# Decoding the third weight group over three steps instead of one, in a fused attention and two-MLP kernel

## The chip, the cores and the metric

The kernel runs on one core of one Trainium2 chip. The metric is the device time of one execution in microseconds; the median of several runs counts. The engines are PE (TensorE, matmuls), DVE (VectorE), ACT (ScalarE), POOL (GpSimd) and SP (SyncE, which issues nearly all DMA transfers). Each works through its own queue in order; between engines they wait on semaphores.

## What is computed

The reference is attention with 4 batches, 8 heads, 576 positions and a head size of 64; heads 0 to 3 see the last 32 positions, heads 4 to 7 every 32nd position. Its output, 2304 tokens by 512, goes through two MLPs:

```
x = attention(q, k, v)                      # 2304 x 512
gate = 1 / (1 + exp(-(x @ w_gate)))         # 512 -> 1536
x = (gate * (x @ w_val)) @ w_out            # 1536 -> 512
h = x @ w_in                                # 512 -> 2048
out = softplus(h) @ w_out2                  # 2048 -> 512
```

All in float32. The kernel splits each float32 operand of the MLPs into a high and a low part and takes three matmuls (high x high, high x low, low x high) for each product.

## The kernel before

**Tiles and loops.** The 2304 tokens are five blocks t = 0 to 4, of 512 tokens and the last of 256. The hidden units of both MLPs are cut into 14 groups g of 256: groups 0 to 5 are the first MLP, with three weight matrices each (m = 0 gate, 1 value, 2 out), groups 6 to 13 the second, with two. A step is a pair (g, t). In `step` (L261) a step of the first MLP sends PE the gate product of this block (`gates`, L161), then the down product of the step before (`down`, L258, and `out1`, L188), then the value product (`values1`, L175); every generator yields after three matmuls, and such a step has 24 yields: 8 gates, 8 down, 8 values. Behind the gates ACT computes a sigmoid for each of two columns (L171). Behind the values DVE multiplies by it (L184, sg), ACT rounds to the high part (L151, gh), DVE takes the low part (L152, gl); the next step's down product reads gh and gl. The down products are taken out of PSUM by ACT in group 0 (L202), by DVE in the others (L204, addition to the accumulator). In PSUM the gate and value products share four buffers, the down products another four.

**Weights.** They come from memory as 64-bit words. A piece (g, m, c) is one half of a matrix, 512 KB; `load_next` (L92) issues its DMA on SP into one of three buffers `raw` and puts the piece into `queue`; `todo` holds the pieces still to be loaded. `decode_steps` (L101) turns the next piece of the queue into its high and low part: two DVE instructions make f (L108, L112), two make e (L117, L122), ACT copies f into the high tile (L121), POOL subtracts (L125) and adds (L126) to make the low tile. Then it calls `load_next`. f and e have two buffers each. There are two sets of weight tiles, taken in turn: group g lies in set g % 2, so tile w00h is the high part of set 0, matrix 0. A piece of group 2 can only be written once its tile has been read for the last time by group 0.

**Order around the change.** The order on every engine is the order in which the code emits instructions. Groups 0 and 1 are taken together: during attention the steps (0,0), (1,0), (0,1), ... (1,2), which fill PE between pieces of attention; then the list `rest` (L271): (0,3), (0,4), (1,4), (1,3), and from there group by group, (2,0) to (13,4). The loop at L543 walks through `rest`, and at a yield j with j % 3 == 2 it may emit one decode. Before the change, `free` allows decodes in (1,3) (all pieces of group 2, six) and, for later groups, from block 1 on (an even share for each step). The pieces of `todo` for groups from 2 on are ordered half by half: all matrices of half 0, then of half 1 (L329). Fifteen pieces are loaded in the attention part, so the first three of group 2 are there early; each later load is issued by a decode.

Of the kernel before, what the change touches and what calls it, by code (L numbers as in the profile page):

```python
# [24 lines left out]
NCC = DM // P  # L25
# [9 lines left out]
GC = 2  # L35
# [7 lines left out]
def tile_sparse_attention_moe_moe2(  # L43
# [17 lines left out]
    NB = len(blocks)  # L61
    NBA = B - 1
    NG = NG1 + NG2
# [23 lines left out]
    queue, todo = [], []  # L87

    def group_mats(g):
        return (0, 1, 2) if g < NG1 else (0, 2)  # L90
# [39 lines left out]
    def decode_next(pools):  # L130
        for _ in decode_steps(pools):
            pass
# [125 lines left out]
    def down(g, t, pools):  # L258
        return (out1 if g < NG1 else out2)(g, t, pools)

    def step(prev, cur, pools, interleave=False):  # L261
        g, t = cur
        if g < NG1:
            yield from gates(g, t, pools, interleave)
            if prev:
                yield from down(*prev, pools)
            yield from values1(g, t, pools)
        else:
            yield from step2(prev, cur, pools)
# [4 lines left out]
    def attention():  # L274
        with ExitStack() as actx:
# [42 lines left out]
            def load_v(i):  # L318
# [7 lines left out]
            todo.extend([(0, 0, 0), (0, 0, 1), (0, 1, 0), (0, 1, 1), (1, 0, 0), (1, 0, 1)])  # L326
            todo.extend([(0, 2, 0), (0, 2, 1), (1, 1, 0), (1, 1, 1), (1, 2, 0), (1, 2, 1)])
            todo.extend(
                (g, m, c) for g in range(2, NG) for c in range(GC) for m in group_mats(g)  # L329
            )  # L330
            load(1)
            load(2)
# [27 lines left out]
            for h in range(2):  # L360
                t = m_loc[h * LQ:(h + 1) * LQ]
# [3 lines left out]
            t = m_str[:SQ].rearrange("p (a b) -> p a b", a=RG)  # L365
# [141 lines left out]
            for u in range(NU + SKEW):  # L507
                t, pos = divmod(u - START, PB)
# [8 lines left out]
                n = 0  # L517
# [12 lines left out]
    with tc.manual_schedule():  # L530
        attention()

        late = ctx.enter_context(tc.tile_pool(name="late", bufs=1))
        pool = lambda name, bufs, **kw: ctx.enter_context(tc.tile_pool(name=name, bufs=bufs, **kw))
        pools = {
            "g": pool("gp2", 2), "t": pool("tp2", 3), "d": pool("decp2", 2), "e": nc.gpsimd,
            "h": pool("ps_h2", 4, space=PSUM), "y": pool("ps_y2", 4, space=PSUM),
        }
        for t in range(NBA, NB):
            acc[t] = late.tile([P, NCC * blocks[t][1]], F32, name=f"acc{t}")  # L540

        prev = (1, NBA - 1)
        for i, cur in enumerate(rest):  # L543
            g, t = cur
            free = (g == 1 and t == 3) or (g > 1 and t > 0)
            n = 0
            if free:
                left = sum(pc[0] == g + 1 for pc in queue + todo)
                n = left if g == 1 else -(-left // max(NB - 1 - t, 1))
            for j, _ in enumerate(step(prev, cur, pools)):  # L550
                if n and j % 3 == 2:
                    n -= 1
                    decode_next(pools)
            while n:
                n -= 1
                decode_next(pools)
            prev = cur
        for _ in down(*prev, pools):
            pass
# [81 lines left out]
```

## Time and profile before

| | |
|---|---|
| runs, us | 983.05, 982.62, 980.76; median 982.62 |
| profiled execution: its time on the core, from first to last instruction (span) | 978.8 us |
| PE busy | 952.3 us (97%) |
| DVE busy | 609.3 us (62%) |
| ACT busy | 404.2 us (41%) |
| POOL busy | 284.1 us (29%) |
| DMA, bytes moved | 62.27 MB, mean 64 GB/s |

For the profiled execution only the span is listed, not the device time of the run around it; the median of the runs lies 3.8 us above this span. Shares of busy time are averages over the whole span; the steps differ, and a stretch is read best from a table of busy times by step and from the engines' timelines.

### The profile page before, as it was taken

To read this page: it belongs to the slowest core of one execution; us is meant where nothing else is said; L and a number is where in the kernel's file an instruction comes from. 1 tells how busy PE (TensorE), PEld (TensorE's weight loads), DVE (VectorE), ACT (ScalarE), POOL (GpSimd) and SP (SyncE) were. 2 spreads that over 40 slices of the span, in tenths; PEclk is the share of its full clock that TensorE was granted. 3 is DMA by queue.
4 is the path that set the end of the run, shared out by engine and by line. 5 is a ranking of instruction groups with operands and counts; after the bars stand their busy time and mean duration, and the time that the engine had idled before them with its cause. 6 is when DMAs were issued, how large, how long until landed. Compare 5 with 4: busy or idle time off the path is not lost.

```text
span 978.8 us, 13104 instructions
## 1 busy us (share of the span) xinstructions
PE 952.3 (97%) x5148; PEld 787.3 (80%) x5148; DVE 609.3 (62%) x969; ACT 404.2 (41%) x729; POOL 284.1 (29%) x256
## 2 busy tenths in 40 slices
PE   8879999999989999999999999999999999999998
PEld 6757778788768888888888887888888888888886
DVE  5888854412767637637636448484859584858554
ACT  3446656642212212212113355454545454455443
POOL 6555533310424204203305534040403031313100
PEclk9979999999979999999999999999999999999999
DMA  8665633100312102102202002020202010200023
GB/s 250 189 194 150 183 98 90 32 7 1 85 45 71 59 1 68 63 1 65 65 1 65 22 1 85 2 76 11 67 20 65 22 64 22 65 22 22 1 78 116
DMA packets 24795, 62.27 MB, mean 64 GB/s; under 512 B 2975, under 2 KB 7071, under 8 KB 24735
## 3 DMA queue, kind: packets, MB, share of 16 engines
q1 hardware_dynamic: 24672, 61.44, 20.7%
q8 instruction: 40, 0.66, 0.3%
q14 instruction: 20, 0.16, 0.1%
q10 hardware_dynamic: 63, 0.01, 0.0%
HBM read 56.71 MB, written 4.72 MB: 63 GB/s over the span
## 4 chain that ended last, share of the span: by engine, by line
PE 87%; DVE 7%; ACT 2%; DMA 1%; issue 1%; POOL 1%; SPq 0%; POOLq 0%; DVEq 0%
PE ps_y L67 12%; PE ps_y L69 12%; PE ps_y L68 11%; PE ps_h L67 6%; PE ps_h L69 6%; PE ps_h L68 6%; PE ps_v L67 5%; PE ps_v L68 5%; PE ps_v L69 5%; PE ps_g L67 4%; PE ps_g L69 4%; PE ps_g L68 4%; DVE f L112 2%; PE ps_s L382 2%; PE ps_o L444 2%; DVE f L108 1%
## 5 line engine op out<-in xcount | busy, mean ns | idle before, releaser
L151 ACT ACTIVATE gh<-sg 128x512 fp32r<-128x512 f32 (+1 forms) x140 | 82.5, 589 | 254.2 <-DVE sg L184 182.9
L253 DVE TENSOR_TENSOR acc<-ps_y,acc 128x512 f32<-128x512 f32 x126 | 86.7, 688 | 89.1 <-PE ps_y L69 88.1
L152 DVE TENSOR_TENSOR gl<-sg,gh 128x512 fp32r<-128x512 f32 (+1 forms) x140 | 100.3, 716 | 54.6 <-ACT gh L151 51.1
L204 DVE TENSOR_TENSOR acc<-ps_y,acc 128x512 f32<-128x512 f32 (+1 forms) x100 | 61.7, 634 | 67.0 <-PE ps_y L69 67.0
L184 DVE TENSOR_TENSOR sg<-ps_v,sg 128x512 f32<-128x512 f32 (+1 forms) x60 | 38.1, 635 | 84.7 <-PE ps_v L69 84.5
L125 POOL TENSOR_TENSOR f<-f,w00h 128x512 f32<-128x512 f32 x12 | 18.5, 1540 | 212.2 <-ACT w00h L121 212.2
L112 DVE SCALAR_TENSOR_TENSOR f<-raw,f 128x512 uint32<-128x512 uint32 x68 | 74.3, 1093 | 2.3
L225 ACT ACTIVATE sg<-ps_h 128x512 f32<-128x512 f32 (+1 forms) x80 | 43.8, 547 | 64.4 <-PE ps_h L69 64.4
L125 POOL TENSOR_TENSOR f<-f,w10h 128x512 f32<-128x512 f32 x12 | 18.3, 1526 | 154.6 <-ACT w10h L121 154.6
L68 PE MATMUL ps_h<-xl,w00h 128*128 128x512 f32 (+1 forms) x160 | 58.9, 368 | 0.0
L67 PE MATMUL ps_h<-xh,w00h 128*128 128x512 f32 (+1 forms) x160 | 58.9, 368 | 0.0
L69 PE MATMUL ps_h<-xh,w00l 128*128 128x512 f32 (+1 forms) x160 | 58.9, 368 | 0.0
L69 PE MATMUL ps_h<-xh,w10l 128*128 128x512 f32 (+1 forms) x160 | 58.9, 368 | 0.0
L68 PE MATMUL ps_h<-xl,w10h 128*128 128x512 f32 (+1 forms) x160 | 58.8, 368 | 0.0
L67 PE MATMUL ps_h<-xh,w10h 128*128 128x512 f32 (+1 forms) x160 | 58.8, 368 | 0.0
L67 PE MATMUL ps_y<-w02h,gh 128*128 128x512 f32 x144 | 56.6, 393 | 0.7 <-ACT gh L151 0.7
L233 DVE SCALAR_TENSOR_TENSOR sg<-ps_h,sg 128x512 f32<-128x512 f32 (+1 forms) x80 | 50.5, 631 | 11.0 <-ACT sg L227 10.6
L67 PE MATMUL ps_y<-w12h,gh 128*128 128x512 f32 x144 | 56.5, 393 | 0.1
L69 PE MATMUL ps_y<-w02h,gl 128*128 128x512 f32 x144 | 56.5, 392 | 0.0
L69 PE MATMUL ps_y<-w12h,gl 128*128 128x512 f32 x144 | 56.5, 392 | 0.0
L68 PE MATMUL ps_y<-w02l,gh 128*128 128x512 f32 x144 | 56.2, 390 | 0.0
L68 PE MATMUL ps_y<-w12l,gh 128*128 128x512 f32 x144 | 56.2, 390 | 0.0
(115 smaller groups left out, 2538.6 us busy)
## 6 DMA issues: line engine op xcount, KB each, us to landing
raw<-in_w_dram SPq DMA_DIRECT2D x68, 512.0 KB, 3.8
out_dram<-acc SPq DMA_DIRECT2D x18, 256.0 KB, 2.0
qt<-in_q_dram SPq DMA_DIRECT2D x8, 324.0 KB, 4.7
qt<-in_q_dram SPq DMA_DIRECT2D x8, 320.0 KB, 4.5
qt<-in_q_dram SPq DMA_DIRECT2D x8, 270.0 KB, 3.9
qt<-in_q_dram SPq DMA_DIRECT2D x8, 256.0 KB, 3.6
vt<-in_vl_dram SPq DMA_DIRECT2D x8, 240.0 KB, 4.8
vt<-in_vl_dram SPq DMA_DIRECT2D x8, 192.0 KB, 3.5
```

The lines of the kernel that those rows point to most:

```text
L67: nc.tensor.matmul(ps, lhsT=lh, rhs=rh, start=first, stop=False)
L68: nc.tensor.matmul(ps, lhsT=lh, rhs=rl, start=False, stop=False)
L69: nc.tensor.matmul(ps, lhsT=ll, rhs=rh, start=False, stop=last)
L112: nc.vector.scalar_tensor_tensor(out=f, in0=high, scalar=0xC0000000, in1=f, op0=ALU.bitwise_and, op1=ALU.bitwise_or,)
L125: pools["e"].tensor_tensor(out=ff, in0=ff, in1=hi.bitcast(F32), op=ALU.subtract)
L151: nc.scalar.activation(out=gh[:, c, 0:n], in_=src, func=AF.Copy)
L152: nc.vector.tensor_tensor(out=gl[:, c, 0:n], in0=src, in1=gh[:, c, 0:n].bitcast(F32), op=ALU.subtract)
L184: nc.vector.tensor_tensor(out=sg, in0=ps[:, 0:n], in1=sg, op=ALU.mult)
L204: nc.vector.tensor_tensor(out=y, in0=ps[:, 0:n], in1=y, op=ALU.add)
L225: nc.scalar.activation(out=sg, in_=ps, func=AF.Abs)
L233: nc.vector.scalar_tensor_tensor(out=sg, in0=ps, scalar=0.0, in1=sg, op0=ALU.max, op1=ALU.add)
L253: nc.vector.tensor_tensor(out=y, in0=ps, in1=y, op=ALU.add)
```

## The change

The condition `free` is replaced. In (0,4) two decodes are emitted, from yield 8 on (behind the gates of that step, at yields 8 and 11); in (1,4) two, at yields 2 and 5; in (1,3) what is left, two, at yields 2 and 5. For later groups the rule and the places stay the same. In `todo` the pieces from group 2 on go matrix by matrix: both halves of a matrix, then the next matrix.

```diff
--- before.py
+++ after.py
@@ -326,7 +326,7 @@
             todo.extend([(0, 0, 0), (0, 0, 1), (0, 1, 0), (0, 1, 1), (1, 0, 0), (1, 0, 1)])
             todo.extend([(0, 2, 0), (0, 2, 1), (1, 1, 0), (1, 1, 1), (1, 2, 0), (1, 2, 1)])
             todo.extend(
-                (g, m, c) for g in range(2, NG) for c in range(GC) for m in group_mats(g)
+                (g, m, c) for g in range(2, NG) for m in group_mats(g) for c in range(GC)
             )
             load(1)
             load(2)
@@ -542,13 +542,16 @@
         prev = (1, NBA - 1)
         for i, cur in enumerate(rest):
             g, t = cur
-            free = (g == 1 and t == 3) or (g > 1 and t > 0)
-            n = 0
-            if free:
-                left = sum(pc[0] == g + 1 for pc in queue + todo)
-                n = left if g == 1 else -(-left // max(NB - 1 - t, 1))
+            left = sum(pc[0] == g + 1 for pc in queue + todo)
+            n, first = 0, 0
+            if (g, t) == (0, NB - 1):
+                n, first = GC, GC * NCC
+            elif g == 1:
+                n = GC if t == NB - 1 else left
+            elif g > 1 and t > 0:
+                n = -(-left // max(NB - 1 - t, 1))
             for j, _ in enumerate(step(prev, cur, pools)):
-                if n and j % 3 == 2:
+                if n and j >= first and j % 3 == 2:
                     n -= 1
                     decode_next(pools)
             while n:
```

How this moves instructions, at three places. In the names, f, e and raw belong to a decode; 128x256 are instructions of block 4; acc_2454 and acc_2455 are the accumulators of blocks 3 and 4.

DVE between the values of (0,3), whose last gl is of 128x512, and those of (1,4). Before, in this place:

```order
L184 TENSOR_TENSOR sg<-ps_v,sg 128x512
L152 TENSOR_TENSOR gl<-sg,gh 128x512
L184 TENSOR_TENSOR sg<-ps_v,sg 128x256
L152 TENSOR_TENSOR gl<-sg,gh 128x256
L184 TENSOR_TENSOR sg<-ps_v,sg 128x256
L152 TENSOR_TENSOR gl<-sg,gh 128x256
```

Now:

```order
L122 SCALAR_TENSOR_TENSOR e<-raw,e 128x512
L108 TENSOR_SCALAR f<-raw 128x512
L112 SCALAR_TENSOR_TENSOR f<-raw,f 128x512
L117 TENSOR_SCALAR e<-f 128x512
L122 SCALAR_TENSOR_TENSOR e<-raw,e 128x512
L184 TENSOR_TENSOR sg<-ps_v,sg 128x256
L152 TENSOR_TENSOR gl<-sg,gh 128x256
L184 TENSOR_TENSOR sg<-ps_v,sg 128x256
L152 TENSOR_TENSOR gl<-sg,gh 128x256
L108 TENSOR_SCALAR f<-raw 128x512
```

The first row is the end of the first decode of (0,4); the second decode follows whole, then the values of (0,4), then the first decode of (1,4). Before, only values stood in this place.

DVE at the end of (1,3), where its values (L184, L152 of 128x512) end the stretch. Before:

```order
L122 SCALAR_TENSOR_TENSOR e<-raw,e 128x512
L204 TENSOR_TENSOR acc_2455<-ps_y,acc_2455 128x256
L108 TENSOR_SCALAR f<-raw 128x512
L112 SCALAR_TENSOR_TENSOR f<-raw,f 128x512
L117 TENSOR_SCALAR e<-f 128x512
L122 SCALAR_TENSOR_TENSOR e<-raw,e 128x512
L184 TENSOR_TENSOR sg<-ps_v,sg 128x512
L152 TENSOR_TENSOR gl<-sg,gh 128x512
```

Now:

```order
L122 SCALAR_TENSOR_TENSOR e<-raw,e 128x512
L108 TENSOR_SCALAR f<-raw 128x512
L112 SCALAR_TENSOR_TENSOR f<-raw,f 128x512
L117 TENSOR_SCALAR e<-f 128x512
L122 SCALAR_TENSOR_TENSOR e<-raw,e 128x512
L204 TENSOR_TENSOR acc_2455<-ps_y,acc_2455 128x256 x4
L184 TENSOR_TENSOR sg<-ps_v,sg 128x512
L152 TENSOR_TENSOR gl<-sg,gh 128x512
L184 TENSOR_TENSOR sg<-ps_v,sg 128x512
```

The last decode stood between the additions of the down product and the first sg of (1,3); now all four additions and the values follow the last decode together.

ACT from the evictions of (0,4)'s down product on. Before:

```order
L202 ACTIVATE acc_2454<-ps_y 128x512 x4
L151 ACTIVATE gh<-sg 128x256 x2
L171 ACTIVATE sg<-ps_g 128x256 x2
L202 ACTIVATE acc_2455<-ps_y 128x256 x4
L151 ACTIVATE gh<-sg 128x256 x2
L121 ACTIVATE w00h<-f 128x512
L171 ACTIVATE sg<-ps_g 128x512
L121 ACTIVATE w01h<-f 128x512
L171 ACTIVATE sg<-ps_g 128x512
L121 ACTIVATE w02h<-f 128x512
L121 ACTIVATE w00h<-f 128x512
L121 ACTIVATE w01h<-f 128x512
```

Now:

```order
L121 ACTIVATE w00h<-f 128x512
L202 ACTIVATE acc_2454<-ps_y 128x512 x2
L121 ACTIVATE w00h<-f 128x512
L202 ACTIVATE acc_2454<-ps_y 128x512 x2
L151 ACTIVATE gh<-sg 128x256 x2
L121 ACTIVATE w01h<-f 128x512
L171 ACTIVATE sg<-ps_g 128x256
L121 ACTIVATE w01h<-f 128x512
L171 ACTIVATE sg<-ps_g 128x256
L202 ACTIVATE acc_2455<-ps_y 128x256 x4
L151 ACTIVATE gh<-sg 128x256 x2
L121 ACTIVATE w02h<-f 128x512
```

The copies L121 now stand between the evictions L202 of (0,4), and ahead of each of the two sigmoids L171 of (1,4); for (1,3) two are left, both of w02h, of which the last row is the first.

## Rows read from the trace of the kernel before

**Rows 1.** The page: its first line, and the granted clock in 40 slices.

```profile
span 978.8 us, 13104 instructions
...
PEclk9979999999979999999999999999999999999999
```

**Rows 2.** Busy us by step: length, PE, PEld, DVE, ACT, POOL, then clock, DMA.

```profile
229.70:240.74 11.04, 11.04 (x73) 10.08 (x73) 2.07 (x4) 4.21 (x8) 0.00 (x0) 1.00 0.01 1
240.74:249.38 8.64, 8.64 (x75) 8.64 (x74) 1.70 (x5) 3.14 (x8) 0.00 (x0) 1.00 0.00 0
249.38:263.18 13.80, 13.80 (x74) 11.89 (x73) 12.97 (x18) 3.28 (x6) 7.58 (x6) 1.00 0.34 83
263.18:291.10 27.92, 21.58 (x73) 15.79 (x72) 18.97 (x24) 4.76 (x8) 9.87 (x7) 0.82 0.22 73
291.10:307.42 16.32, 16.32 (x73) 13.51 (x72) 11.62 (x16) 3.50 (x6) 5.83 (x4) 1.00 0.20 65
```

**Rows 3.** PE's timeline at the step (2,0): start us, us, engine, line, operands.

```profile
266.13 0.39 PE L68 MATMUL ps_g<-xl,w00h 128*128 128x512 f32 x1
268.72 0.79 PE L69 MATMUL ps_g<-xh,w00l 128*128 128x512 f32 x1 [2.20 <-POOL w00l L126]
...
276.02 0.79 PE L67 MATMUL ps_y<-gh,w12h 128*128 128x512 f32 x1 [3.15 <-ACT gh L151]
277.77 0.80 PE L68 MATMUL ps_y<-gl,w12h 128*128 128x512 f32 x1 [0.96 <-DVE gl L152]
```

**Rows 4.** DVE's timeline, steps (0,3) to (2,0).

```profile
231.11 0.69 DVE L152 TENSOR_TENSOR gl<-sg,gh 128x512 fp32r<-128x512 f32 x1 [0.70 <-ACT gh L151]
239.57 0.42 DVE L184 TENSOR_TENSOR sg<-ps_v,sg 128x256 f32<-128x256 f32 x1 [7.76 <-PE ps_v L69]
240.48 0.43 DVE L152 TENSOR_TENSOR gl<-sg,gh 128x256 fp32r<-128x256 f32 x1 [0.48 <-ACT gh L151]
...
241.85 0.42 DVE L152 TENSOR_TENSOR gl<-sg,gh 128x256 fp32r<-128x256 f32 x1 [0.48 <-ACT gh L151]
...
250.83 0.42 DVE L108 TENSOR_SCALAR f<-raw 128x512 uint32<-128x512 uint32 x1
...
253.08 1.52 DVE L108 TENSOR_SCALAR f<-raw 128x512 uint32<-128x512 uint32 x1
...
257.40 1.52 DVE L108 TENSOR_SCALAR f<-raw 128x512 uint32<-128x512 uint32 x1
...
274.62 0.68 DVE L184 TENSOR_TENSOR sg<-ps_v,sg 128x512 f32<-128x512 f32 x1
276.00 1.72 DVE L152 TENSOR_TENSOR gl<-sg,gh 128x512 fp32r<-128x512 f32 x1 [0.70 <-ACT gh L151]
```

**Rows 5.** POOL's timeline, steps (1,3) and (2,0).

```profile
252.77 1.53 POOL L125 TENSOR_TENSOR f<-f,w00h 128x512 f32<-128x512 f32 x1 [45.16 <-ACT w00h L121]
254.39 1.36 POOL L126 TENSOR_TENSOR w00l<-f,e 128x512 fp32r<-128x512 f32 x1
257.04 1.60 POOL L125 TENSOR_TENSOR f<-f,w01h 128x512 f32<-128x512 f32 x1 [1.29 <-ACT w01h L121]
...
275.90 1.26 POOL L126 TENSOR_TENSOR w02l<-f,e 128x512 fp32r<-128x512 f32 x1
```

**Rows 6.** PE's timeline: the first down product in (1,4), and in (1,3).

```profile
243.62 0.28 PE L67 MATMUL ps_y<-gh,w02h 128*128 128x256 f32 x1
...
254.84 0.28 PE L67 MATMUL ps_y<-gh,w12h 128*128 128x256 f32 x1
```

**Rows 7.** ACT's timeline, steps (1,4) and (1,3).

```profile
242.44 0.38 ACT L171 ACTIVATE sg<-ps_g 128x256 f32<-128x256 f32 x1 [0.62 <-PE ps_g L69]
...
244.53 0.38 ACT L202 ACTIVATE acc<-ps_y 128x256 f32<-128x256 f32 x1 [0.28 <-PE ps_y L69]
...
252.01 0.63 ACT L121 ACTIVATE w00h<-f 128x512 fp32r<-128x512 f32 x1 [1.56 <-DVE f L112]
```

**Rows 8.** The tile view of the raw words, its last line.

```profile
DMA to landing us min/median/max: 3.6/3.8/6.7
```

## What the change should do to the time

> **What bounds the kernel now.** I read the page's span and slices first [rows 1]: TensorE's granted clock is at full almost everywhere, with one dip early, in the attention part, and one in the twelfth of the 40 slices, some 269 to 294 us into the span. The second dip is where the change works, so I cut that stretch by step with the busy-time table [rows 2]; the step borders are the starts of the first matmul of each step in PE's timeline. A step is written (group, token block); its sequence on PE is gates, then the down product of the step before, then values. In (0,4), (1,4) and (1,3) PE is busy all the time (11.04, 8.64 and 13.80 us). Step (2,0) takes 27.92 us of which PE works 21.58, at a granted clock of 0.82; (2,1), right behind it and with the same 72 matmuls, takes 16.32 us at clock 1.00. So (2,0) alone holds 27.92 - 16.32 = 11.60 us more than it needs: 27.92 - 21.58 = 6.34 us of idle PE, and 5.26 us of matmuls that run slowly.
>
> PE's own timeline shows the three holes [rows 3]: 2.20 us before 268.72 (waits for w00l, the last weights of the gates, written by POOL), 3.15 us before 276.02 (waits for gh) and 0.96 us before 277.77 (waits for gl), 6.31 together. The matmul at 266.13 takes 0.39 us and the one behind the hole 0.79: the clock fell after PE had idled, to the lower of its two levels, 1.2 GHz, and came back to 2.4 later.
>
> Why PE waits is in DVE's timeline [rows 4]. The six decodes (four DVE instructions each: L108, L112, L117, L122) stand in a row from 250.83 on. The first takes 253.08 - 250.83 = 2.25 us, the next 257.40 - 253.08 = 4.32, because POOL works on the decode before (L125 and L126, 252.77 to 254.39 + 1.36 = 255.75, a pair of about 3.0 us [rows 5]) while DVE's L108 and L112 run. With the four additions of the down product among them, the product sg of (1,3) comes at 274.62 and gl at 276.00, while PE could have used both at 263.18 + 5.46 = 268.64, behind the 24 matmuls of its gates (as many took 249.38 to 254.84 in (1,3) [rows 2, 6]). DVE is thus the bound of this one stretch: 12.97 us busy of 13.80 in (1,3), against 2.07 of 11.04 and 1.70 of 8.64 in the two steps before [rows 2].
>
> **The change, part by part.**
> *Removed from (1,3):* four decodes, 4 x 4.32 = 17.3 us of DVE time, with their ACT copies and POOL pairs. Two stay there.
> *Added to (0,4) and (1,4):* two decodes each. A pair costs DVE 2.25 + 4.32 = 6.57 us if POOL is idle as the first begins, the nearest rows. The other bound is 2 x 4.32 = 8.64.
> I walk through it with the trace's times for PE, since PE isn't to wait.
> (0,4): DVE is free at 231.11 + 0.69 = 231.80 [rows 4]. Decodes A, B: to 234.05 and 238.37. A's ACT copy has to follow the last matmul that reads w00, that is the gates of (0,4), and stands in ACT's queue behind their sigmoid anyway. The product sg of (0,4) needs its matmuls only at 239.57 [rows 4], so 1.2 us are spare. POOL's pair for B starts 3.96 us after B's start, by the trace (257.04 after 253.08) at 238.01, to 241.0; gl, whose turn would be 0.91 us after sg, so 240.48, waits for it to some 0.5 us. The last gl, at 241.85 + 0.42 = 242.27 before, comes at 242.8. The down product starts at 243.62 [rows 6]: no wait.
> (1,4): decodes C, D from 242.8 to 245.05 and 249.37. ACT's order is: copy C, sigmoid, copy D, sigmoid, four evictions, gh. Copy D waits for D's L112, some 3.25 us after D's start, 248.30; then 0.63 + 0.38 + 4 x 0.38 us [rows 7] make gh possible at 250.85, to 251.3. POOL's pair for D lasts to 252.0, and the first gl waits for it, to 252.4; sg, gh and gl of the second column follow 0.42 us each, to 253.7. The down product needs the first at 254.84 [rows 6] and the second 0.4 us later. Spare: 1.1 us, the tightest place. The late sigmoids are harmless: their PSUM banks (four) are wanted again at 249.38 and 252.11, and come free at about 245.0 and 249.3.
> (1,3): decodes E, F from 253.7 to 255.95 and 260.27; four additions of 0.42 to 261.95; sg, gh, gl twice to about 266.1. Needed at 268.64: spare 2.5 us.
> (2,0): w00 is complete with POOL's pair B, 241.0, against 263.18; w01 with D, 252.0, against 274.1; w02 with F, 262.9, against (2,1). So no hole of [rows 3] is left and the step should be a steady one, 16.32 us.
> *Words and their queue:* three raw buffers hold words A, B and C from the attention part on. D's load is issued on SP once A is decoded, 234.05, and lands 3.8 us later, at most 6.7 [rows 8], so by 240.8; D reads it at 245.05. E and F have more time. SP has nothing else to issue here. So nothing; if the 4 us of cover were gone, D and all that waits on it would be late by what is missing.
> *Loading matrix by matrix:* same 68 loads, same sizes; beyond group 2 all pieces of a group are decoded by its third decoding step in either order, and read from the next group's first step on, so nothing. For group 2 it is what lets A and B write w00 alone, free after the gates of (0,4), when w01 and w02 are still read.
>
> **Sum:** profiled span 978.8 less 11.60 gives 967.2. Between the span and the median of the runs shown, 982.62, lie 3.8 us (980.76 to 983.05 are 1.9 to 4.2); these stay. 982.62 - 11.60 = **971.0 us**, -1.2%. Full activity of PE in all other steps of the stretch leaves no second gain. Bounds of the unknown costs: a new hole at the down product of (1,4) of 0 to 2.20 us, the nearest hole in [rows 3], with slow matmuls in proportion (5.26/6.34 = 0.83 per us idle): 0 to 4.0 us. I take 0, as two decodes per 16.32 us step run so behind (2,1) [rows 2], though that step is longer than (1,4); 4.0 is kept for the range.
>
> **Rivals.**
> *gl stands behind POOL each time.* At 276.00 gl took 1.72 us against 0.69 elsewhere, POOL's L126 running from 275.90 on [rows 4, 5]. If each of the four gl of the two short steps loses a whole POOL instruction, up to 1.60 us, the delay is 4 x 1.60 - 1.6 (counted above) = 4.8 us; 1.1 is spare, so PE idles 3.7 us and loses 3.1 more at the low clock: 971.0 + 6.8 = 977.8. Against it: POOL works only some 6 us of each short step, and two gl fall outside by the walk. The Trainium skill (SBUF — State Buffer, section Who interferes with whom) states this lock: a VectorE instruction with two SBUF inputs and a GpSimd one that reads SBUF exclude each other, and the second "fully blocks". The 1.72 us row agrees with it; taken for all four gl it gives this rival's 977.8, while the walk, in which two of them meet POOL for part of an instruction, gives 971.0.
> *The clock does not come back.* If the low clock behind 268 us were not a result of the idle time, only 6.34 us would be won: 976.3. Against it: clock 1.00 in every step around where PE has no hole [rows 2].
> *Nothing moves.* If the decodes were still held back until (1,3) by a wait on a tile, 982.6. Against it: each destination is last read before its decode, as walked.
> *Slower: ACT's queue as the new bound.* Copy C and D now stand ahead of the sigmoids of (1,4), the evictions and gh; what DVE is late with D, all of these are late, then PE's down product. It decides from 1.1 us of lateness on; each further one costs 1.83 us with the clock, so it takes 1.1 + 6.3 = 7.4 us of lateness to be no better than before. Six decodes at 4.32 us each give only 4.1 more there (two of the fast ones, 2.07 us each), 1.83 x (4.1 - 1.1) = 5.6 us, 976.6; with twice the needed lateness, 14.8 us, the time would be 971.0 + 1.83 x 13.7 = 996. For it: (1,4) now has 6.57 + 1.70 = 8.27 us of DVE work in 8.64. Against it: (0,4) hands on only 0.5 us of lateness, and (1,3) has 2.5 us to make good what is left.
>
> **How the numbers follow.** No new hole 0.84; gl behind POOL 0.08; clock 0.03; nothing moves 0.02; ACT's queue 0.03. The likeliest, with the runs' own spread (980.76 to 983.05) and up to half of the new hole, spans 969 to 973.5; I give 968.8 to 975.5, which takes in the 4.0 us bound. 0.3% (2.9 us) is about what a measurement of this kernel can tell from no change. Faster: 0.84 + 0.08 + 0.03 = 0.95; same 0.02; slower 0.03.
>
> **What would show it.** Right: PE without a hole from (0,4) to (2,1), (2,0) at 16.3 us, clock 1.00 throughout; decodes on DVE in three pairs of some 6.6 us; POOL's first L125 near 234. Wrong: a hole in PE before the first ps_y matmul of (1,4) or (1,3), released by gl or gh; a clock below 1.00 there; gl of 128x256 well over 1 us twice in each short step; or a decode that waits for a load.

## The result, and the profile after

| | before | after |
|---|---|---|
| runs, us | 983.05, 982.62, 980.76, 982.49 | 968.46, 969.73, 968.13, 968.60 |
| median | 982.56 | 968.53 |
| span of the profiled execution | 978.8 | 966.5 |

The ratio of the times is 0.987, with an interval of 0.9856 to 0.9885: 14.0 us faster, where 11.6 were forecast. The time lies 2.5 us under the forecast 971.0 and 0.3 under the low end of the range. In a later comparison (after_again) the same kernel took 970.16 (4 runs) against 981.81 (19 runs), 0.9878 (0.9862 to 0.9894), 11.65 us.

The page of the kernel after, its first line, the busy times and the granted clock, against [rows 1] and the table of the section on the profile before:

```profile
span 966.5 us, 13105 instructions
...
PE 944.8 (98%) x5148; PEld 783.6 (81%) x5148; DVE 606.1 (63%) x969; ACT 403.5 (42%) x729; POOL 284.4 (29%) x256
...
PEclk9979999999999999999999999999999999999999
```

The dip in the twelfth slice is gone; the dip in the attention part stands as it was. PE's busy time falls by 7.5 us with the same matmuls: 21.58 - 16.32 = 5.3 of that is (2,0), where none of them runs at the lower level of the clock now, and the rest lies in the attention part.

Busy time by step, with the columns of [rows 2] (the first three borders are those of before, and two steps of 16.32 us follow; the steps themselves begin 0.47 us sooner than these borders, (2,0) at 262.71):

```profile
229.70:240.74 11.04, 11.04 (x72) 10.08 (x72) 8.46 (x13) 5.15 (x10) 5.75 (x4) 1.00 0.29 88
240.74:249.38 8.64, 8.64 (x73) 8.55 (x72) 7.44 (x11) 3.32 (x10) 4.18 (x3) 1.00 0.22 73
249.38:263.18 13.80, 13.80 (x74) 11.89 (x73) 10.73 (x18) 3.60 (x8) 7.67 (x6) 1.00 0.35 115
263.18:279.50 16.32, 16.32 (x74) 13.51 (x73) 5.54 (x9) 2.46 (x4) 0.00 (x0) 1.00 0.00 0
279.50:295.82 16.32, 16.32 (x74) 13.51 (x73) 11.62 (x17) 3.50 (x6) 5.83 (x4) 1.00 0.20 65
```

DVE's 12.97 us of (1,3) and 18.97 of (2,0) before are now spread: 8.46, 7.44, 10.73 and 5.54. PE is busy in every microsecond, at clock 1.00, and (2,0) takes 16.32 us instead of 27.92. Those 11.60 us are the change. The two profiled spans differ by 12.3: PE also reaches (0,4) 0.47 us earlier (the first sg of (0,4) on DVE starts at 239.10 instead of 239.57), out of the attention part, which the change doesn't touch, and the last 0.2 us lie behind (2,0).

DVE's timeline after, where [rows 4] stood; the columns are the same:

```profile
231.25 0.42 DVE L108 TENSOR_SCALAR f<-raw 128x512 uint32<-128x512 uint32 x1
...
233.51 1.52 DVE L108 TENSOR_SCALAR f<-raw 128x512 uint32<-128x512 uint32 x1
...
241.53 0.43 DVE L152 TENSOR_TENSOR gl<-sg,gh 128x256 fp32r<-128x256 f32 x1 [0.49 <-ACT gh L151]
241.88 0.42 DVE L108 TENSOR_SCALAR f<-raw 128x512 uint32<-128x512 uint32 x1
...
247.85 0.69 DVE L122 SCALAR_TENSOR_TENSOR e<-raw,e 128x512 f32<-128x512 uint32 x1
...
249.72 0.42 DVE L152 TENSOR_TENSOR gl<-sg,gh 128x256 fp32r<-128x256 f32 x1 [0.85 <-ACT gh L151]
...
250.97 0.62 DVE L152 TENSOR_TENSOR gl<-sg,gh 128x256 fp32r<-128x256 f32 x1 [0.48 <-ACT gh L151]
251.51 0.41 DVE L108 TENSOR_SCALAR f<-raw 128x512 uint32<-128x512 uint32 x1
...
262.91 0.69 DVE L184 TENSOR_TENSOR sg<-ps_v,sg 128x512 f32<-128x512 f32 x1 [0.57 <-PE ps_v L69]
264.30 0.69 DVE L152 TENSOR_TENSOR gl<-sg,gh 128x512 fp32r<-128x512 f32 x1 [0.70 <-ACT gh L151]
```

Pairs of decodes start at 231.25, 241.88 and 251.51. The last gl of (1,3) ends at 264.99, and the sg before it waits for PE: DVE has gone from leading the wait to following it. PE's down products start here, in (1,4), in (1,3) and in (2,0):

```profile
243.15 0.28 PE L67 MATMUL ps_y<-gh,w02h 128*128 128x256 f32 x1
...
254.37 0.28 PE L67 MATMUL ps_y<-gh,w12h 128*128 128x256 f32 x1
...
268.15 0.39 PE L67 MATMUL ps_y<-gh,w12h 128*128 128x512 f32 x1
```

No row has a bracket: no wait. The second column's gl is read four matmuls after these starts, 0.48 us in the first two and 0.91 in the third. So the last gl of (0,4), done at 241.96, has 1.67 us to spare, that of (1,4), done at 251.59, has 3.26, and that of (1,3) has 4.07. The least spare time is in (0,4), not in (1,4).

POOL's timeline after, pairs A and D of the walk, where [rows 5] stood:

```profile
233.22 1.51 POOL L125 TENSOR_TENSOR f<-f,w00h 128x512 f32<-128x512 f32 x1 [26.08 <-ACT w00h L121]
234.81 1.36 POOL L126 TENSOR_TENSOR w00l<-f,e 128x512 fp32r<-128x512 f32 x1
...
248.09 1.60 POOL L125 TENSOR_TENSOR f<-f,w01h 128x512 f32<-128x512 f32 x1 [1.29 <-ACT w01h L121]
249.77 1.53 POOL L126 TENSOR_TENSOR w01l<-f,e 128x512 fp32r<-128x512 f32 x1
```

### The profile page after: what moved, and what is told of

The parts are those of the page before. It is cut to its first block, busy times and chain, and to the rows that moved or that the text cites. A ratio compares the mean times of both kernels' runs of the same rounds, so it can differ in the third digit from the quotient of the medians.

```text
span 966.5 us, 13105 instructions
## 1 busy us (share of the span) xinstructions
PE 944.8 (98%) x5148; PEld 783.6 (81%) x5148; DVE 606.1 (63%) x969; ACT 403.5 (42%) x729; POOL 284.4 (29%) x256
## 4 chain that ended last, share of the span: by engine, by line
PE 89%; DVE 6%; ACT 2%; DMA 1%; POOL 1%; issue 1%; SPq 0%; POOLq 0%; DVEq 0%
PE ps_y L67 12%; PE ps_y L69 12%; PE ps_y L68 11%; PE ps_h L68 7%; PE ps_h L69 7%; PE ps_h L67 7%; PE ps_v L67 5%; PE ps_g L67 5%; PE ps_v L68 5%; PE ps_v L69 5%; PE ps_g L68 5%; PE ps_g L69 5%; PE ps_s L382 2%; DVE f L112 1%; PE ps_o L444 1%; DVE f L108 1%
## 5 line engine op out<-in xcount | busy, mean ns | idle before, releaser
L152 DVE TENSOR_TENSOR gl<-sg,gh 128x512 fp32r<-128x512 f32 (+1 forms) x140 | 99.7, 712 | 55.0 <-ACT gh L151 51.4
L184 DVE TENSOR_TENSOR sg<-ps_v,sg 128x512 f32<-128x512 f32 (+1 forms) x60 | 38.1, 635 | 73.5 <-PE ps_v L69 73.4
L112 DVE SCALAR_TENSOR_TENSOR f<-raw,f 128x512 uint32<-128x512 uint32 x68 | 72.4, 1065 | 2.3
L233 DVE SCALAR_TENSOR_TENSOR sg<-ps_h,sg 128x512 f32<-128x512 f32 (+1 forms) x80 | 50.5, 631 | 10.5 <-ACT sg L227 9.9
```

The lines of the kernel that those rows point to most:

```text
L112: nc.vector.scalar_tensor_tensor(out=f, in0=high, scalar=0xC0000000, in1=f, op0=ALU.bitwise_and, op1=ALU.bitwise_or,)
L152: nc.vector.tensor_tensor(out=gl[:, c, 0:n], in0=src, in1=gh[:, c, 0:n].bitcast(F32), op=ALU.subtract)
L184: nc.vector.tensor_tensor(out=sg, in0=ps[:, 0:n], in1=sg, op=ALU.mult)
L233: nc.vector.scalar_tensor_tensor(out=sg, in0=ps, scalar=0.0, in1=sg, op0=ALU.max, op1=ALU.add)
```

## The experiments

The step (2,0), from its first gate matmul to that of (2,1), measures each of these better than the whole time does; it is read from PE's timeline of each profiled run.

| kernel | (2,0), us | median (runs) | ratio to before (interval) |
|---|---|---|---|
| before | 27.92 | 981.14 (25) | |
| the order of loading alone | 27.88 | 982.64 (10) | 1.0011 (1.0 to 1.0023) |
| large holes filled | 27.97 | 980.91 (10) | 0.9999 (0.9989 to 1.001) |
| all holes filled | 26.83 | 979.62 (10) | 0.9984 (0.9972 to 0.9996) |
| no POOL work for group 2 | 16.82 | 969.87 (4) | 0.9892 (0.9868 to 0.9917) |
| two steps, not three | 20.55 | 973.72 (4) | 0.9925 (0.9907 to 0.9943) |
| after | 16.32 | 970.16 (4) | 0.9878 (0.9862 to 0.9894) |

"All holes filled", "two steps" and "after" stand against 981.81 (19 runs of before on their chip), the rest against 981.14.

**The order of loading alone** (label e_order), on the kernel before:

```diff
-                (g, m, c) for g in range(2, NG) for c in range(GC) for m in group_mats(g)
+                (g, m, c) for g in range(2, NG) for m in group_mats(g) for c in range(GC)
```

> The kernel before with the loading order alone changed to matrix by matrix; the six decodes stay in (1,3). Theory (the decodes' sum on DVE sets the end of the stall): w00 is complete with POOL's second pair, so the first hole of PE (2.20 us before 268.72) goes, but gh and gl of (1,3) come as late as before, so PE waits longer for gh and the step (2,0) still takes some 27.9 us: 982.6 us, within 1 us. Rival (each hole counts by itself): 2.20 us less, 980.4 us.

Waits of PE between 200 and 300 us, by what was waited for: total, times, longest:

```profile
PE ps_y L67 <- ACT gh L151: 7.2, 1, 7.2
PE ps_y L68 <- DVE gl L152: 1.0, 1, 1.0
```

The hole of 2.20 us before the gates' last weights [rows 3] is gone, as w00 is now decoded first, and the hole before the down product has grown from 3.15 to 7.24 us. The step is as long as before. Holes don't add up each by itself: they all wait for one sum, DVE's six decodes and the values behind them.

**The spread alone** (e_spread), on the kernel after:

```diff
-                (g, m, c) for g in range(2, NG) for m in group_mats(g) for c in range(GC)
+                (g, m, c) for g in range(2, NG) for c in range(GC) for m in group_mats(g)
```

> The changed kernel with the old loading order (half by half); decodes in three pairs. B then writes w01 in (0,4) and C writes w02 in (1,4), both still being read: ACT's copy of B waits for the first value column of (0,4), some 2 us later than now, C's for the down product of (0,4), some 3 us later, and the sigmoids and evictions of (1,4) stand behind them in ACT's queue. Theory (the spread alone brings the gain, lateness is taken up by what is spare before the down product of (1,4), 2.8 us in the trace): within 1 us of the changed kernel, 968 to 970 us. Rival (the loading order is needed): a hole at the down product of (1,4) of 2 us or more, 971 us or more.

It took 978.47 (10 runs), 0.9972 (0.9958 to 0.9986). PE's waits from 200 to 300 us:

```profile
PE ps_y L69 <- POOL w02l L126: 2.5, 1, 2.5
PE ps_v L69 <- POOL w01l L126: 2.5, 1, 2.5
PE ps_y L67 <- ACT w02h L121: 0.3, 1, 0.3
```

The expectation had overlooked what this order means. The second piece is then w01, decoded in (0,4) ahead of the values of (0,4), and the third w02, ahead of its down product. Those products read group 2's weights instead of group 0's, and wait for the decode that writes them: (0,4) takes 15.60 us instead of 11.22, (1,4) 13.46 instead of 8.64, and (2,0) 16.32. So the time says what these waits cost; the kernel no longer computes what it should. The order of loading, worth nothing alone, is the condition of the spread: only w00 is free in (0,4).

**Large holes filled** (e_fill), on the kernel before: matmuls that nobody reads, 10 and 20 of them, where PE waits in (2,0).

```diff
+                if cur == (2, 0) and j in (3, 7):
+                    if j == 3:
+                        ps_f = pools["y"].tile([P, TB], F32, tag="y", name="ps_f")
+                    for _ in range(10 if j == 3 else 20):
+                        nc.tensor.matmul(
+                            ps_f, lhsT=xh[:, 0, 0:P], rhs=xh[:, 0, 0:TB], start=True, stop=True
+                        )
```

> The kernel before with 10 idle matmuls of 512 columns ahead of the second gate column of (2,0) and 20 ahead of its first down product, so that PE works through most of the holes and the clock should stay at 2.4 GHz; their result is not used. Theory A (idle time and slow clock add up, as the prediction split them): the 5.26 us of slow matmuls go, 977.3 us. Theory B (DVE's chain sets when PE goes on, and most slow matmuls lie under its waits): the last gl of (1,3) still comes at about 279.7 us; only the matmuls behind it run faster, some 1.4 us less, 981.2 us. If the clock falls all the same: 982.6 us.

PE's timeline of it:

```profile
265.84 2.43 PE L555 MATMUL ps_f<-xh 128*128 128x512 f32 x10
...
271.10 4.69 PE L555 MATMUL ps_f<-xh 128*128 128x512 f32 x20
...
277.80 0.50 PE L68 MATMUL ps_y<-gl,w12h 128*128 128x512 f32 x1 [1.29 <-DVE gl L152]
...
279.06 0.79 PE L67 MATMUL ps_y<-gh,w12h 128*128 128x512 f32 x1 [0.53 <-ACT gh L151]
```

Two holes are full, and 1.29 and 0.53 us are left; behind these the matmuls take 0.79 us, the lower level of the clock, as before. So this didn't tell what the clock is worth, and was done again with more.

**All holes filled** (e_fill2): the edit of e_fill with more matmuls and a third place.

```diff
-                if cur == (2, 0) and j in (3, 7):
+                if cur == (2, 0) and j in (3, 7, 8):
...
-                    for _ in range(10 if j == 3 else 20):
+                    for _ in range({3: 10, 7: 29, 8: 4}[j]):
```

> The kernel before with idle matmuls also in the holes that were left in the first such run, 29 instead of 20 ahead of the down product of (2,0) and 4 more behind its first column, so that PE hardly idles until 279.7 us. Theory (DVE's last gl sets when PE goes on, the slow matmuls behind it are all that the clock costs): clock at 2.4 GHz throughout the step, (2,0) ends 1.4 us earlier, 1.0 to 1.8 us under the kernel before. Rival (slow clock costs 5.26 us): 5.3 us under it. If the clock falls all the same: as the kernel before.

PE waits for nothing between 200 and 300 us. Busy time of most of (2,0), with the columns of [rows 2]:

```profile
263.18:280.00 16.82, 16.73 (x73) 13.10 (x72) 14.61 (x17) 4.13 (x7) 9.63 (x7) 1.00 0.35 114
```

DVE's timeline, the last gl of (1,3), and PE's, the matmul that reads it:

```profile
278.78 0.69 DVE L152 TENSOR_TENSOR gl<-sg,gh 128x512 fp32r<-128x512 f32 x1 [0.70 <-ACT gh L151]
```

```profile
279.52 0.50 PE L68 MATMUL ps_y<-gl,w12h 128*128 128x512 f32 x1
```

The clock is at 1.00 throughout, and the step still takes 26.83 us: of the 11.60 us only 1.1 belong to the clock (the medians give 2.2, with an interval of 0.4 to 2.7). The rest is DVE's: this gl is used at 279.52, where PE, which starts the first gate at 262.82, could have used it 28 matmuls later, at 262.82 + 28 x 0.227 = 269.18, 10.3 us sooner.

**No POOL work for group 2** (e_nopool), on the kernel before: the low halves of group 2's weights aren't made.

```diff
+        if g != 2:
             pools["e"].tensor_tensor(out=ff, in0=ff, in1=hi.bitcast(F32), op=ALU.subtract)
             nc.gpsimd.tensor_tensor(out=lo, in0=ff, in1=ef, op=ALU.add)
```

> The kernel before, with POOL's subtraction and addition left out for the six pieces of group 2, so the low halves of these weights are not computed. Theory (a decode takes DVE 4.32 us because POOL works beside it): all six decodes take 2.25 us, they end at about 264.3, the last gl of (1,3) comes at about 269.7, a hole of at most 0.5 us is left: 971 us, though all six decodes still stand in one step. Rival (it is the number of decodes in the step, whatever each takes beside POOL): (2,0) stays at 27.9 us, 982.6 us.

DVE's timeline, the start of the first decode, the second of the six, and the last gl of (1,3):

```profile
255.15 0.42 DVE L108 TENSOR_SCALAR f<-raw 128x512 uint32<-128x512 uint32 x1
...
257.40 0.42 DVE L108 TENSOR_SCALAR f<-raw 128x512 uint32<-128x512 uint32 x1
257.86 0.69 DVE L112 SCALAR_TENSOR_TENSOR f<-raw,f 128x512 uint32<-128x512 uint32 x1
...
273.48 0.69 DVE L153 TENSOR_TENSOR gl<-sg,gh 128x512 fp32r<-128x512 f32 x1 [0.70 <-ACT gh L152]
```

All six decodes now take 2.25 us: L108 0.42 instead of 1.52, L112 0.69 instead of 1.66. The stall is gone but for one wait of 0.2 us. In the kernel before, the first decode starts at 250.83 [rows 4], and the last gl of (1,3) is this row:

```profile
279.01 0.69 DVE L152 TENSOR_TENSOR gl<-sg,gh 128x512 fp32r<-128x512 f32 x1 [0.70 <-ACT gh L151]
```

From the first decode to the end of this gl DVE takes 279.70 - 250.83 = 28.9 us before and 274.17 - 255.15 = 19.0 here: 9.9 us are lost beside POOL. The second and third decode lose 4.32 - 2.25 = 2.07 each, the other three, which take 3.7 to 4.0 us, less, and one gl loses 1.0 (1.72 instead of 0.69). PE could have used the last gl at 263.18 + 28 x 0.227 = 269.54, so it came 10.2 us late before, and comes 0.3 late here. Without the time lost to POOL six decodes in (1,3) would have done. (The edit also takes away the wait for w00l, but e_order shows that this alone is worth nothing.)

**Two steps, not three** (e_two), on the kernel after:

```diff
-            if (g, t) == (0, NB - 1):
-                n, first = GC, GC * NCC
-            elif g == 1:
+            if g == 1:
                 n = GC if t == NB - 1 else left
```

> The changed kernel with no decode in (0,4): two in (1,4), four in (1,3). Theory (the time follows DVE's lateness with the last gl of (1,3) against the 269.55 us at which PE could use it, 10.15 us before the change): the six decodes now start 8.5 us earlier than before the change, the last gl comes some 3.3 us too late, the step (2,0) loses that and up to 1.4 us of slow matmuls behind it: 3.3 to 4.8 us above the changed kernel, 972 to 973.5 us. Rival (two steps are as good as three): no hole, 968.5 us.

PE's waits from 200 to 300 us, and then, from DVE's timeline, the last gl of (1,3):

```profile
PE ps_y L68 <- DVE gl L152: 0.8, 2, 0.6
PE ps_y L67 <- ACT gh L151: 0.8, 2, 0.5
```

```profile
270.66 0.69 DVE L152 TENSOR_TENSOR gl<-sg,gh 128x512 fp32r<-128x512 f32 x1 [0.69 <-ACT gh L151]
```

Four decodes in (1,3) are too many: the last gl, done at 271.35, comes 2.6 us after PE could have used it (262.38 + 28 x 0.227 = 268.74), (2,0) takes 4.23 us more, and the time is 3.6 us more than that of the kernel after in the same comparison. The waits are but 1.6 us of it; matmuls at the lower level of the clock and the short pieces of work between the holes make the rest.

**The kernel after again** (after_again), for a second measurement beside these:

> The changed kernel once more, beside the others of this job, so that they are compared on one chip: 968 to 970 us.

The time is in the table, and (2,0) takes 16.32 us again.

**The place called tightest, made late** (e_late), on the kernel after: ten reductions on DVE behind the second decode of (1,4).

```diff
+        scr = late.tile([P, 5], F32, name="scr")
...
+                    if cur == (1, NB - 1) and n == 0:
+                        for _ in range(10):
+                            nc.vector.tensor_reduce(
+                                out=scr, in_=xh[:, 0, 0:480].bitcast(F32).rearrange("p (a b) -> p a b", a=5),
+                                axis=AX.X, op=ALU.max,
+                            )
```

> The changed kernel with ten DVE reductions of 128x480 (0.53 us each, 5.3 us) put between the second decode of (1,4) and the values of that step; their result is not used. By the prediction (1.1 us spare, 1.83 us for each us beyond): 4.2 x 1.83 = 7.7 us more than the changed kernel, 976.2 us. By the changed kernel's trace (the last gl of (1,4) comes 3.26 us ahead of its use): a hole of some 2 us at the down product of (1,4), and 2.0 us (if only the wait counts) to 3.7 us (if slow matmuls come on top) more: 970.5 to 972.2 us.

It took 980.73 (10 runs), 0.9994 (0.9984 to 1.0004): about 10.6 us above the kernel after. DVE's timeline, PE's at the down product of (1,3), and the busy time of the steps (2,0) and (2,1), in this order:

```profile
249.07 6.85 DVE L560 TENSOR_REDUCE scr<-xh 128x5 f32<-128x480 f32 x10
...
257.97 0.42 DVE L152 TENSOR_TENSOR gl<-sg,gh 128x256 fp32r<-128x256 f32 x1 [0.48 <-ACT gh L151]
```

```profile
256.75 0.38 PE L67 MATMUL ps_y<-gh,w12h 128*128 128x256 f32 x1 [1.54 <-ACT gh L151]
...
257.99 0.39 PE L67 MATMUL ps_y<-gh,w12h 128*128 128x256 f32 x1 [0.27 <-ACT gh L151]
...
259.05 0.41 PE L67 MATMUL ps_y<-gh,w12h 128*128 128x256 f32 x1
```

```profile
267.90:284.42 16.52, 16.52 (x74) 13.51 (x72) 5.82 (x9) 2.46 (x4) 0.00 (x0) 1.00 0.01 4
284.42:300.94 16.52, 16.52 (x74) 13.51 (x72) 11.63 (x16) 3.50 (x6) 5.85 (x4) 1.00 0.20 64
```

The place is where it was forecast, the price isn't. The down product of (1,3) takes 255.05 to 262.40, 7.35 us instead of 257.25 - 254.37 = 2.88: 4.5 us for 6.85 - 3.26 = 3.6 us put in beyond the spare time. By this trace the last gl, done at 258.39, is 2.9 us late, as PE could have read it at 255.05 + 0.48 = 255.53. Of the 4.5 us 1.8 are waits, and 1.5 are the 14 matmuls behind that gl, 0.41 us instead of 0.28: from 258.45 to 261.61 the granted clock is 0.50, and they take 3.16 us instead of 14 x 0.12 = 1.68.

There is no price per microsecond in this. Late by 10.2 us, the last gl cost the kernel before 11.6; by 2.6, e_two 4.2; by 2.9, this kernel 4.5; and by 10.3 with the clock at 1.00 (e_fill2) 10.5. In these traces lateness costs its own length and, where the clock falls, 1.4 to 1.6 us once.

The other 6 us were not meant: every later step is 16.52 us long instead of 16.32, with no wait in it. The ratio alone would have confirmed the price of the prediction, (6.85 - 1.1) x 1.83 = 10.5, by accident. The expectation also took 0.53 us for a reduction, as the trace of before has it for four shapes together (L393, 534 ns); for 128x480 alone it has 654 ns.

**Where gh and gl stand.** The tile `scr` had moved them by 32 bytes in SBUF. Three kernels followed that: e_late2, as e_late with `scr` padded to 128 bytes; e_pad, the kernel after with the 20-byte tile and no reductions; e_align, the kernel after with 64 bytes more among the constants of the attention part, whose own gh and gl are moved by that.

```diff
-        scr = late.tile([P, 5], F32, name="scr")
+        scr = late.tile([P, 32], F32, name="scr")[:, 0:5]
...
+        scr = late.tile([P, 5], F32, name="scr")
+        nc.vector.memset(scr, 0.0)
...
+            pad = const.tile([P, 16], F32, name="pad")
+            nc.gpsimd.memset(pad, 0.0)
```

> The run with ten added reductions once more, with their result in a tile of 128 bytes per partition instead of 20, so that the tiles allocated behind it (gh, gl, sg, f, e of the late part) stand at multiples of 128 bytes as in the changed kernel; in the first such run they stood 32 bytes further, and matmuls that read gh or gl came every 0.233 us instead of 0.227. The reductions took 6.85 us there, not 5.3. Theory (place of gh and gl in memory makes the difference of the later steps): the lateness alone is left, 6.85 - 3.26 us of wait and slow matmuls, some 4.3 us over the changed kernel, 973 to 974 us. Rival (lateness goes on through the later steps): 980 us again.

> The changed kernel with a tile of 20 bytes per partition that is only cleared once, which puts gh and gl of the late part 32 bytes off; no reductions. Theory (the place of gh and gl): some 6 us over the changed kernel, 974 to 976 us, with no hole in PE. Rival: as the changed kernel, 968 to 970 us.

> The changed kernel with 64 bytes of padding ahead of the attention part's tiles, so that gh and gl of that part stand at a multiple of 128 bytes; they stand 64 bytes off, and the down products that read them (six, of 24 matmuls) come every 0.233 us. Theory: 0.227 us there, up to 1.0 us less where PE sets the time, 968 to 969.5 us; that is near what the runs' own spread hides, so the spacing of the matmuls decides. Rival (64 bytes off costs nothing): spacing and time as before.

| kernel | median (runs) | ratio to before, 980.74 (13) |
|---|---|---|
| e_late2 | 981.35 (10) | 1.0005 (0.9995 to 1.0014) |
| e_pad | 975.77 (4) | 0.9945 (0.9925 to 0.9965) |
| e_align | 969.26 (4) | 0.9879 (0.986 to 0.9898) |

The costliest groups of PE by form, of the kernel after and of e_pad; the last numbers before the idle time are the busy time in us and the mean of one in ns. After:

```profile
L67 PE MATMUL ps_y<-w12h,gh 128*128 128x512 f32 x144 | 56.5, 392 | 0.0
L68 PE MATMUL ps_y<-w02l,gh 128*128 128x512 f32 x144 | 56.2, 390 | 0.0
```

And e_pad:

```profile
L67 PE MATMUL ps_y<-w12h,gh 128*128 128x512 f32 x144 | 57.1, 396 | 0.0
L68 PE MATMUL ps_y<-w02l,gh 128*128 128x512 f32 x144 | 56.8, 395 | 0.0
```

For e_late2 973 to 974 was expected, and 981.35 measured; for e_pad 974 to 976, and 975.77 measured. e_pad does no more work than one clearing of the tile and takes 5.6 to 7.2 us more than the kernel after (970.16, 968.53). From the start of (2,0) to the end the two profiled executions take 974.9 - 264.53 = 710.4 and 966.5 - 262.71 = 703.8 us. Some 5 ns for each of 1,248 matmuls of 128x512 with gh or gl behind the attention part (six such groups of 144, and 384 in groups 2 to 5) are 6.2 us of these 6.6. In e_late2 the means are 395 to 397, so a multiple of 128 bytes isn't the condition. The addresses of gh in the built programs are 188544 with the short matmuls, 188576 (e_late, e_pad) and 188672 (e_late2) with the long; in the attention part 212800 with the long and 212864 (e_align) with the short (there the additions behind the down product follow one another by 1.36 us instead of 1.40). The weights and x lie 128 past a multiple of 256, and so do 188544 and 212864, the two with the short matmuls; the other three don't. Whether the place counts against the other operand or by itself wasn't tried, nor was any other distance. e_align shows it for the steps in the attention part too, but there it makes no difference in time that can be told.

**POOL's addition on DVE during attention** (e_dve), on the kernel after:

```diff
-        nc.gpsimd.tensor_tensor(out=lo, in0=ff, in1=ef, op=ALU.add)
+        pools["e"].tensor_tensor(out=lo, in0=ff, in1=ef, op=ALU.add)
```

> The changed kernel with the addition that ends a decode (L126) on DVE instead of POOL for the twelve decodes of the attention part. DVE is over 90% busy from 50 to 110 us there. Theory (POOL's 1.28 us of addition holds DVE up by more than the 0.68 us that DVE would need for it): 1 to 6 us less, 963 to 969 us. Rival (12 x 0.68 = 8.2 us more work on the busiest engine): up to 8 us more, 969 to 977 us.

It took 971.83 (4 runs), 0.9902 (0.9883 to 0.9921), 2.6 us more than e_align on the same chip: no gain, as the rival of its expectation had it. No version ran faster than the kernel after by more than the measurement can tell.

## Why the prediction was right, and where not

**The stall and its size: right.** (2,0) was forecast at 16.32 us, clock 1.00, and it is. The cause, six decodes in a row on DVE that POOL's work makes longer, is shown by e_nopool (without that work the stall is gone) and e_order (the holes move, the end doesn't). The 4.32 us were taken for each removed decode, 17.3 for four; that holds for two of the six, and three take 3.7 to 4.0.

**The walk: right in its places, too cautious at one.** With PE 0.47 us earlier, the forecast ends of the pairs become 237.9, 248.9 and 259.8; measured are 237.91, 248.54 and 258.16. The first POOL row starts at 233.22, forecast near 234. The last gl of (0,4) was to end at 242.8 - 0.47 = 242.3, and ends at 241.96. For (1,4) 253.7 - 0.47 = 253.2 was forecast, and 251.59 measured: 3.26 us of spare time to the matmul that reads it, where the walk gives 1.6 (its 1.1 was counted to the first matmul of the down product). Of the 1.6 us between, 0.45 are D's start, 244.13 instead of 245.05 - 0.47. Another 0.7 are ACT's queue, from its timeline:

```profile
247.38 0.63 ACT L121 ACTIVATE w01h<-f 128x512 fp32r<-128x512 f32 x1 [3.36 <-DVE f L112]
...
248.19 1.20 ACT L202 ACTIVATE acc<-ps_y 128x256 f32<-128x256 f32 x4
249.24 0.45 ACT L151 ACTIVATE gh<-sg 128x256 fp32r<-128x256 f32 x1
```

gh starts 1.86 us after copy D, where 0.63 + 0.38 + 4 x 0.38 = 2.53 were counted. The last 0.7 are the step that failed: "POOL's pair for D lasts to 252.0, and the first gl waits for it". With gh that early, this gl starts at 249.72, in the gap before POOL's second instruction, and takes 0.42 us; POOL's instruction takes 1.53 then, instead of 1.36. The second gl takes 0.62 for 0.42, which gives 0.2 of all this back.

The walk also called the wrong place the tightest: by its own numbers the gl of (0,4) came at 242.8 against 243.62, 0.8 us, and the trace after has the least spare time there too.

The lock that the Trainium skill states (SBUF — State Buffer, section Who interferes with whom; the shared ports are "an exclusive lock" there, and the words "fully blocks" stand beside VectorE's two-port modes) bore on two of the four short gl, by 0.28 (0.70 for 0.42) and 0.20 us, and in one case on POOL. It depends on who comes first, as the same section says, so the rival that took it for all four gl by whole instructions (977.8) didn't come about.

**"5.26 us of matmuls that run slowly": not a term of its own.** The sum 6.34 + 5.26 holds as a total, since both vanish, but e_fill2 shows that at full clock the step is 1.1 us shorter, not 5.26: PE would have waited for DVE instead. What was built on that split was wrong with it: "slow matmuls in proportion" to the idle time, and "each further one costs 1.83 us with the clock". Measured were the lateness itself and 1.6 us once (e_late, e_two).

**The 3.8 us between the span and the median, "these stay": mis-sized.** The forecast 971.0 is a span of 967.2 and these 3.8; measured were 966.5 and, to the median, 2.0. In every run of the kernel after, the time is 1.9 to 2.0 us above the span (968.46 for 966.5, 969.73 for 967.8). The other 1.9 of the 3.8 us were the distance of the profiled execution of before, 980.76 by that, to its median; where such a distance arises was seen in e_nopool, whose profiled run took 3.8 us more than its other three: its (2,0) begins 4.3 us later than in the profile of before, with no wait of PE in the steps ahead of it, so the loss lies in the attention part. A low profile was thus put with a middling median. Before's medians on other chips are 980.74 to 981.81, and 981.81 - 11.60 = 970.21 is the 970.16 of the second measurement. The interval of the first one, 11.3 to 14.1 us, holds 11.6 as well, so its 14.0 are best read as 11.6 of the change and about 2.4 of differences between runs. Of the miss of 2.5 us 1.8 are this term and 0.7 the span (0.47 of it ahead of (0,4), 0.2 behind (2,0)); the range should have had some 2 us below for it.

**"Loading matrix by matrix": right, and underrated.** Cost: nothing (e_order). Its use was named, w00 alone in (0,4), but it was not put among the ways in which the change could fail; e_spread shows it is the condition of the rest.

**The rivals.** The clock came back, and the decodes did move. ACT's queue didn't become the bound: 6.85 us of lateness at (1,4) cost 4.5 us, so the rival was real in its place, with 3.26 us of spare time instead of the walk's 1.6. With two steps, of two and four decodes, 4.2 us are lost (e_two); other ways to share them between two weren't tried.

## What to carry to other kernels

Where an engine waits in several holes, look for the one sum behind them and compare it with when its last result could be used; filling or moving holes, or the clock in them, changes little until that sum is shorter. A decode took DVE 2.25 us alone and 4.32 beside POOL's work; such work is best put where DVE would idle, and spread over steps whose spare time is counted to the matmul that reads the result. What lies between a span and the time of a run is measured on runs that have both, and not taken from a median of other runs. A duration is taken from rows of the same shape, not from a mean over several.

## What was not expected of the hardware

A tile of 20 bytes, put ahead of gh and gl, made each 128x512 matmul that reads them some 5 ns longer and the kernel 6 to 7 us slower, with no wait of PE from 200 to 300 us, where the steps behind (1,3) grew from 16.32 to 16.52: an experiment that adds a tile can move what it measures.
